# Three two-bank PSUM slots, token sums per batch, a gate in steps and expert pages begun ahead of w2: one change to a linear-attention and expert-routing kernel

## The chip, the cores and the metric

The kernel runs on one core of a Trainium2 chip. Times are microseconds (us) on the device. A kernel is timed several times and the median counts; each timed kernel runs on the same chip as the kernel before, in turns. Each set of runs fell on one of several chips, and the kernel before needs 514 to 516 us on some of them and 519 to 520 us on others.

Engine names as in the profile: PE is TensorE's matmul stream and PEld its weight loads, DVE is VectorE, ACT is ScalarE, POOL is GpSimd, SP is SyncE. A name with a q behind it (SPq, ACTq) is that engine's queue when it issues a transfer. L156 is line 156 of the kernel that is shown. The clock (PEclk) is the granted share of TensorE's full clock.

## The reference, cut to what matters

Attention with random features comes first (batch 8, 8 heads, 576 tokens, head dimension 64, 128 features). Its output, 4608 tokens of 512, goes through a gate that picks one of 8 experts for each token, where a token may have to stay with the expert of the token before it. Then come that expert's two layers.

```python
def phi(x):                                   # x: q or k, scaled
    h = x @ omega.T - sum(x * x) / 2
    return exp(h - max(h)) / sqrt(m)          # the maximum is over the 128 features of one token and head
kv  = einsum('bhsm,bhsd->bhmd', phi(k), v)    # sums over the 576 tokens of a batch
z   = sum(phi(k), axis=2)
out = einsum('bhsm,bhmd->bhsd', phi(q), kv) / (einsum('bhsm,bhm->bhs', phi(q), z) + 1e-6)
# gate: e = argmax(x @ w_gate), or the expert of the token before, by a local gate
h = maximum(x @ w1[e], 0);  y = p[e] * (h @ w2[e])
```

Two things in it shape the kernel. No Q work of a batch can start before all its tokens are in `kv`. And no token can be routed before the gate has seen the tokens ahead of it, so the tokens are routed in two epochs of four batches each and laid out in pages of 128 tokens of one expert.

## The kernel before

K work goes by pairs of batches, nine units a pair: one for the 64-token remainders of both batches, then four of 128 tokens for each batch. The nine Q units of a pair are woven between the K units of the next pair. The weights w1 and w2 arrive in 64 pieces of 512 KB, each loaded to a staging buffer and cast to bf16 by ACT, POOL or DVE. These are the parts that the change touches (cuts marked `...`):

```python
wst  = pool("wst", 3)                              # staging buffers of the weight pieces
ps_t = pool("ps_t", 2, space=PSUM)                 # transposes: one bank each
ps_p = pool("ps_p", 2, space=PSUM)                 # projections: two banks each
ps_k = pool("ps_k", 2, space=PSUM)                 # token sums, later y: one bank each

def k_tile(kb_r, v_view):                          # one K unit
    tp = ps_t.tile(...)  ; 4 transposes            # PE
    kt = copy(tp)                                  # DVE
    pj = ps_p.tile(...)  ; 4 matmuls               # PE
    mx = reduce_max(pj)                            # DVE  (kmx)
    kp = exp(pj)                                   # ACT
    va = v * exp(-mx)                              # POOL
    return kp, va

def main(bb, r):                                   # unit r of batch bb of the pair
    ...
    kp, va = k_tile(...)
    q_tile(...)                                    # 4 transposes of q, copy by ACT
    kv_acc(kst8["kv"], kp, va, 0, 128, False, r == 3)   # 8 matmuls into two sum banks held over the batch
    if r == 3:
        kv_done(P, bb)                             # copy of the sums, 4 transposes, 8 gate matmuls, 3 small copies

for P in range(1, NP):
    for i in range(9):
        ku[i](); qu[i](); load_w(1, "AP")          # K unit, Q unit of the pair before, one piece of w1
    if P == 2: gates[0] = gate(0)                  # routing of the first epoch, in one block
    if P == 3: scatter(*gates[0])                  # 18 indirect writes of the page list, on POOL
...
for i in range(9): qu[i](); load_w(2, "PA")        # last Q units, w2
load_w(32, "PVA")
gates[1] = gate(1)
for ep in range(2):
    ...                                            # list read, 18 pages: gather (POOL), transpose by DMA (SP),
    for i in range(18): page(...)                  # layer 1, relu (ACT), 8 transposes, layer 2, write-back (POOL)
rest(0)                                            # overflow pages, behind a register and a branch
```

The softmax here doesn't subtract the row's maximum and nothing guards it: scores larger than these inputs give would overflow.

## Time and profile before

| | kernel before |
|---|---|
| median, all its runs beside the changed kernel | 514.38 us (4 runs, 513.25 to 515.57) |
| span of the profiled run | 511.2 us |
| busy: PE, DVE, ACT, POOL | 62%, 41%, 34%, 43% |
| mean granted clock | 0.731 |
| first maximum reduction (kmx) starts | 13.3 us |
| the K units of pairs 1, 2, 3 start (first kmx of each) | 55.1, 112.2, 183.3 us |
| last kmx starts | 237.6 us |
| cast of w2: first starts, last ends | 242.8, 302.6 us |
| last of the 36 regular pages is scaled (y) | 482.3 us |

The kmx records make good marks: there is just one for each of the 36 K units, on one engine, in order. I use them, the first and last w2 cast and the last y to cut every run into the same seven stretches. No engine is anywhere near 100% of the span. The averages hide that the stretches have different limits, so the stretches are what has to be read; the prediction shows them for this kernel.

### The profile page before, as it was taken

Reading aid. Unit: us, or ns where it says so; the run is one execution under the profiler, and the core shown is the slowest. Engines: PE = TensorE matmul, PEld = TensorE weight load, DVE = VectorE, ACT = ScalarE, POOL = GpSimd, SP = SyncE. Lnnn points to the kernel's source line nnn. Section 1 sums busy time; section 2 is a strip of 40 time slices with the busy share of each in tenths; the row PEclk is TensorE's granted clock in tenths of the full one; section 3 lists DMA queues with packets and bytes.
Section 4 is the critical chain, followed back from the end, with each engine's and each line's share of the span. In section 5 each row is a group of like instructions: output and inputs, shape, how many; then the busy total and the mean of one; then the engine's idle time right before and its main releaser. Section 6 shows DMA issues by size and latency. Waiting matters only on the chain.

```text
span 511.2 us, 7103 instructions
## 1 busy us (share of the span) xinstructions
PE 317.5 (62%) x2305; PEld 180.6 (35%) x2305; DVE 209.1 (41%) x504; ACT 172.2 (34%) x267; POOL 221.8 (43%) x222
## 2 busy tenths in 40 slices
PE   1455666657573463385532205759999999999633
PEld 0344434335352342163222202324444444444211
DVE  6334454544557653474447410122333233333202
ACT  1256274646453054345562111012222222222100
POOL 3464343345435048822322137753454545453321
PEclk9999565656575565556555556679999999999958
DMA  9949648967796930240798851143444444443110
GB/s 210 330 165 290 248 160 308 240 229 248 257 268 248 324 127 22 103 146 21 248 318 296 289 162 37 42 115 105 124 127 132 120 127 106 133 121 86 74 37 34
DMA packets 82486, 86.62 MB, mean 169 GB/s; under 512 B 39520, under 2 KB 64608, under 8 KB 82448
## 3 DMA queue, kind: packets, MB, share of 16 engines
q1 hardware_dynamic: 72048, 66.91, 43.4%
q0 software_dynamic: 6112, 14.40, 8.8%
q10 hardware_dynamic: 4288, 4.82, 2.8%
q8 instruction: 22, 0.36, 0.3%
q14 instruction: 16, 0.13, 0.1%
HBM read 67.21 MB, written 14.77 MB: 160 GB/s over the span
## 4 chain that ended last, share of the span: by engine, by line
PE 26%; DMA 10%; issue 9%; POOL 6%; ACT 5%; DVE 2%; POOLq 0%; SPq 0%; ACTq 0%; DVEq 0%
PE kv L626 13%; DMA wstage<-in_moe_w_dram 8%; PE pj L615 7%; PE tp L621 3%; ACT h L618 3%; POOL page_list L535 2%; POOL w_all L121 2%; POOL xg L606 1%; DMA lia<-page_list 1%; PE pj L154 1%; DVE kmx L157 1%; ACT kp L159 1%; ACT qp L265 1%; DMA page_list<-meta,posi 0%; PE kv L175 0%
## 5 line engine op out<-in xcount | busy, mean ns | idle before, releaser
L615 PE MATMUL pj<-w_all,xt 128*128 x304 | 80.3, 401 | 42.9 <-DMA xt<-xg 42.9
L618 ACT ACTIVATE h<-pj 128x1024 bf16<-128x1024 f32 x38 | 38.9, 1024 | 159.2 <-PE pj L615 159.2
L626 PE MATMUL kv<-w_all,ht 128*128 x304 | 75.0, 391 | 5.2 <-DVE ht L623 5.2
L164 POOL TENSOR_TENSOR va<-stage,ek 128x512 bf16<-128x512 f32 x32 | 33.5, 1048 | 80.4 <-ACT ek L162 34.6
L606 POOL DMA_INDIRECT xg<-x_tok,ix x36 | 37.5, 1042 | 51.2 <-DMA xt<-xg 47.6
L121 POOL CAST w_all<-wstage 128x1024 bf16<-128x1024 f32 x30 | 31.3, 1046 | 57.2 <-DMA wstage<-in_moe_w_dram 56.3
L615 PEld LDWEIGHTS <-xt 128*128 128x128 bf16 x304 | 29.6, 102 | 73.6 <-DMA xt<-xg 41.8
L157 DVE TENSOR_REDUCE kmx<-pj 128x8 f32<-128x1024 f32 x36 | 43.9, 1222 | 25.7 <-PE pj L154 24.9
L175 PE MATMUL kv<-va,kp 128*128 128x65 bf16 (+1 forms) x320 | 22.8, 230 | 42.4 <-POOL va L164 41.6
L159 ACT ACTIVATE kp<-pj 128x1024 bf16<-128x1024 f32 x36 | 36.8, 1023 | 36.0 <-DVE kmx L157 35.9
L623 DVE COPY ht<-tp 128x1024 bf16<-128x1024 bf16 x38 | 26.1, 687 | 53.4 <-PE tp L621 53.2
L626 PEld LDWEIGHTS <-ht 128*128 128x128 bf16 x304 | 29.9, 99 | 49.3 <-DVE ht L623 18.7
L535 POOL DMA_INDIRECT page_list<-meta,posi x36 | 35.8, 995 | 24.3 <-DVE meta L523 14.3
L154 PE MATMUL pj<-om_bd,kt 128*128 128x256 bf16 x144 | 35.5, 395 | 14.1 <-ACT kp L159 9.5
L117 ACT CAST w_all<-wstage 128x1024 bf16<-128x1024 f32 x30 | 31.4, 1046 | 34.7 <-DMA wstage<-in_moe_w_dram 31.2
L265 ACT ACTIVATE qp<-pj 128x1024 bf16<-128x1024 f32 x32 | 32.5, 1023 | 20.8 <-PE pj L261 20.8
L175 PEld LDWEIGHTS <-kp 128*128 128x128 bf16 (+1 forms) x320 | 19.6, 120 | 49.3 <-issue 39.1
L629 DVE TENSOR_SCALAR y<-kv,lia 128x512 f32<-128x512 f32 x18 | 13.5, 751 | 48.5 <-PE kv L626 48.5
L245 DVE RECIPROCAL rd<-pj 128x8 f32<-128x8 f32 x36 | 7.3, 203 | 62.1 <-PE pj L275 54.7
L275 PE MATMUL pj<-kvb,qp 128*128 128x74 bf16 x256 | 22.6, 246 | 15.2 <-ACT qp L265 9.6
L629 DVE TENSOR_SCALAR y<-kv,lib 128x512 f32<-128x512 f32 x18 | 13.5, 751 | 37.1 <-PE kv L626 37.1
L171 ACT COPY qt<-tp 128x512 bf16<-128x512 bf16 x32 | 18.6, 589 | 26.7 <-PE tp L170 26.6
(181 smaller groups left out, 463.2 us busy)
## 6 DMA issues: line engine op xcount, KB each, us to landing
wstage<-in_moe_w_dram SPq DMA_DIRECT2D x64, 512.0 KB, 4.7
stage<-in_k_dram SPq DMA_DIRECT2D x8, 1024.0 KB, 7.3
stage<-in_q_dram SPq DMA_DIRECT2D x8, 1024.0 KB, 8.8
stage<-in_v_dram SPq DMA_DIRECT2D x8, 1024.0 KB, 11.1
x_tok<-xr ACTq DMA_DIRECT2D x16, 256.0 KB, 4.4
str_k<-in_k_dram SPq DMA_DIRECT2D x8, 128.0 KB, 4.0
str_q<-in_q_dram SPq DMA_DIRECT2D x8, 128.0 KB, 4.2
str_v<-in_v_dram SPq DMA_DIRECT2D x8, 128.0 KB, 4.4
```

Of the source, the lines that this page charges most:

```text
L121: nc.gpsimd.tensor_copy(dst, st)
L154: nc.tensor.matmul(pj[:, 2 * hp:2 * hp + 2, :].rearrange("p a d -> p (a d)"), lhsT=kt[:, hp], rhs=om_bd, start=True, stop=True)
L157: nc.vector.tensor_reduce(mx, pj, axis=AX, op=Alu.max)
L159: nc.scalar.activation(kp, pj, Act.Exp, scale=scale)
L164: nc.gpsimd.tensor_tensor(va[:, :, 0:Dh], v_view, ek.to_broadcast([128, 8, Dh]), op=Alu.mult)
L175: nc.tensor.matmul(kv[h // 4][:, (h % 4) * 65:(h % 4) * 65 + 65], lhsT=kp[lo:lo + n, h, :], rhs=va[lo:lo + n, h, :], start=first and h % 4 ...
L265: nc.scalar.activation(qp, pj, Act.Exp, scale=scale)
L535: s_ = nc.gpsimd.indirect_dma_start(out=plist, out_offset=bass.IndirectOffsetOnAxis(ap=posi[:, t:t + 1], axis=0), in_=meta[:, t, :], in_of ...
L606: nc.gpsimd.indirect_dma_start(out=xg, out_offset=None, in_=src, in_offset=bass.IndirectOffsetOnAxis(ap=ix[:, i:i + 1], axis=0), bounds_ch ...
L615: nc.tensor.matmul(h_ps[:, c, :], lhsT=xt[:, dc, :], rhs=w1_all[:, ds(ev + (dc * F + c * 512), 512)], start=(dc == 0), stop=(dc == DC - 1))
L618: nc.scalar.activation(h, h_ps.rearrange("p a (f c) -> p (a f) c", c=128), Act.Relu)
L626: nc.tensor.matmul(y_ps, lhsT=ht[:, f], rhs=w2_all[:, ds(ev + f * D, D)], start=(f == 0), stop=(f == FC - 1))
```

## The change

Its intent: a third slot for projections, so that PE waits less for evacuations; token sums made in one go after a batch, so that PE doesn't stand at a sum after every unit; the gate's chain of small steps hidden among K and Q units; the scatters hidden under the w2 load; and the first expert layer of some pages, which needs only w1, ahead of the rest of w2. The core of the diff (the gate's other `yield`s, renamed helpers and moved lines are cut):

```diff
-    wst = pool("wst", 3)
-    ps_t = pool("ps_t", 2, space=bass.MemoryType.PSUM)
-    ps_p = pool("ps_p", 2, space=bass.MemoryType.PSUM)
-    ps_k = pool("ps_k", 2, space=bass.MemoryType.PSUM)
+    wst = pool("wst", 2)
+    ps_t = pool("ps_t", 1, space=bass.MemoryType.PSUM)
+    ps_p = pool("ps_p", 3, space=bass.MemoryType.PSUM)
+    ps_k = pool("ps_k", 1, space=bass.MemoryType.PSUM)
...
-    def kv_acc(kv, kp, va, lo, n, first, last):
-        for h in range(H): ...
+    def kv_half(tiles, g):
+        kv = ps_k.tile([128, 4, Dh + 1], F32, name="kv")
+        for i, (kp, va, lo, n) in enumerate(tiles):
+            for h in range(4):
+                nc.tensor.matmul(kv[:, h, :], lhsT=kp[lo:lo + n, 4 * g + h, :], rhs=va[lo:lo + n, 4 * g + h, :], ...)
+        return kv
...
             for g in range(2):
-                nc.scalar.copy(kvb[:, 4 * g:4 * g + 4, 0:65], kv[g][:, 0:260]...)
+                nc.scalar.copy(kvb[:, 4 * g:4 * g + 4, 0:Dh + 1], kv_half(tiles, g))
...
-        return [rem] + [main(bb, r) for bb in range(2) for r in range(4)]
+        return [main(0, r) for r in range(4)] + [rem] + [main(1, r) for r in range(4)]
...
-    load_pair_rem(0)
     load_main(0)
...
+        if P == 3:
+            ga = gate(0)                       # now a generator
...
-            load_w(1, WENG)
+            load_w(1 if P < 3 else 2, "P")
+            if P == 3:
+                next(ga, None)
+                next(ga, None)
...
         qu[i]()
-        load_w(2, "PA")
-    load_w(32, "PVA")
+        load_w(4, "PAV")
+        scatter(0, 2 * i)
+        scatter(0, 2 * i + 1)
...
+    for i in range(NEP):
+        queue.append((lia, i) + hidden(fetch(i, [ixa_], [x_tok[0]]), eia, i))   # first layer
+        for _ in range(3):
+            next(gb_, None)                    # gate(1)
+        out_one(WH - i // 4)                   # second layer, WH = 7 pages behind at most
+        if i >= 5:
+            for t in range(2 * (i - 5), min(2 * (i - 5) + 2, 18)):
+                scatter(1, t)
```

The second layer's y moves from the sum banks to a projection slot. `kp` and `va` get six buffers, since all units of a batch are now kept until its sums.

## The prediction

> **What bounds the kernel now.** I read the page's slices first, then a table of busy time by stage, then the chain of waits, then the waits of TensorE (PE). The slices show three regimes.
>
> ```profile
> PE   1455666657573463385532205759999999999633
> PEclk9999565656575565556555556679999999999958
> DMA  9949648967796930240798851143444444443110
> ```
>
> One digit is 12.8 us. In the first 24 PE is half busy at half clock and no engine is full; from about slice 26 PE is 90% busy or more at full clock: those are the expert pages, which are PE-bound. I cut the run at the marks that instructions give: phase 0 (K only) to 56, pairs 1 and 2 of K with Q to 107 and 160, the routing gate alone to 181, pair 3 to 243, the Q tail to 268, the rest of the w2 load to 302, a slow start of the pages to 340, full pages to 482, overflow pages.
>
> ```profile
> core 0: us, PE busy (x) PEld busy (x) DVE busy (x) ACT busy (x) POOL busy (x), PEclk, DMA share, GB/s
> 13.00:56.00 43.00, 23.72 (x218) 17.15 (x217) 17.21 (x25) 19.41 (x43) 19.70 (x17) 0.92 0.90 276
> 56.00:107.00 51.00, 31.40 (x304) 21.25 (x303) 25.51 (x56) 28.43 (x51) 22.25 (x20) 0.57 0.75 237
> 107.00:160.00 53.00, 33.90 (x336) 22.62 (x334) 27.68 (x62) 29.13 (x53) 22.82 (x21) 0.60 0.80 255
> 160.00:181.00 21.00, 8.29 (x58) 7.09 (x56) 16.03 (x60) 1.92 (x4) 5.42 (x4) 0.50 0.68 231
> 181.00:243.00 62.00, 33.66 (x322) 21.97 (x319) 30.68 (x71) 30.15 (x54) 34.23 (x33) 0.56 0.25 86
> 243.00:268.00 25.00, 11.25 (x126) 6.26 (x124) 11.84 (x37) 14.41 (x16) 7.12 (x7) 0.50 0.86 286
> 268.00:302.00 34.00, 6.11 (x32) 5.45 (x32) 17.05 (x73) 7.98 (x9) 6.71 (x7) 0.50 0.84 278
> 302.00:340.00 38.00, 18.13 (x74) 7.78 (x75) 5.22 (x11) 4.10 (x4) 27.83 (x28) 0.68 0.25 59
> 340.00:482.00 142.00, 139.08 (x791) 65.47 (x790) 46.10 (x66) 32.78 (x32) 63.73 (x62) 0.98 0.41 114
> ```
>
> Three stretches do little for their length. 160 to 181: the gate, DVE 16 of 21 us, nothing beside it. 243 to 302: 32 pieces of w2, DMA 85% busy, PE waiting for the data. 302 to 340: GpSimd (POOL) 28 of 38 us busy with list scatters and gathers while pages drip in. Pair 3 took 62 us against 51 and 53, with POOL up by 12 us: the 18 scatters of the first epoch. The chain agrees for w2 and after; it could be followed back only to 205.5 us.
>
> ```profile
> 268.47 5.96 DMA wstage<-in_moe_w_dram
> 274.48 1.05 POOL w_all L121
> ...
> 297.08 4.62 DMA lia<-page_list
> ```
>
> Each w2 piece is a transfer of 4 to 6 us and then a cast, and the first page waits for a list read issued behind all of them. PE's waits name what the change goes for:
>
> ```profile
> PE pj L615 <- DMA xt<-xg: 42.9, 4, 23.7
> PE kv L175 <- POOL va L164: 41.6, 24, 6.0
> ```
>
> The first is the page start. In the second an in-order PE sits at a token-sum matmul until POOL has scaled v; 18.9 of the 41.6 us fall in pair 3, behind the scatters, 12.4 in phase 0, only 5.9 and 4.4 in pairs 1 and 2.
>
> **What the Trainium skill says.** "Perfetto Trace Analysis", Optimization Strategy, advises interleaving regimes that have different limits; gate, scatter, w2 load and first layer are such regimes, and the table shows them one after another. The same section says that a repeating bubble can mean that PSUM has no room for the next tile. "TensorE: Matmul & The Clock Gate", Part 1, says that the clock is half or full and that idle windows bring it down; the trace agrees (0.50 to 0.60 in K/Q, 0.98 in the pages). "PSUM — Partial Sum Buffer", PSUM bank collisions, says that two engines may not be in one bank at once; so a one-bank slot makes its writer and reader take turns. After the change all eight banks are 1 transpose + 3x2 projection + 1 sum bank. "DMA: Bandwidth & Descriptors", Anatomy of one DMA, fits (for GpSimd-issued transfers) 2.0 us + bytes/436 GB/s: 3.2 us for 512 KB. These are issued by SyncE, yet the shortest w2 landing here is 3.4 us; the median with three in flight is 4.7.
>
> **The change part by part.**
>
> *Gate and scatters moved.* The gate's 21 us leave the path and its DVE work goes between units of pair 3. DVE was 31 of 62 us there, so it has room, but the in-order engines meet chains of PE and DVE: I charge 8 us. The scatters (1.0 us plus 0.3 of issue, 18 of them, 23 us) go to the Q tail, where POOL is 7 of 25 busy beside w2. Pair 3 then resembles pair 2.
>
> *Three slots, sums late.* A K unit holds a slot for 1.0 (matmuls) + 1.2 (max) + 1.0 (exp), a Q projection 0.6 + 1.0, a numerator 0.7 + 1.1: 6.6 us per unit pair, 3.3 on two slots, 2.2 on three. Measured are 51/9 = 5.7 and 53/9 = 5.9, so slots are not the only limit; ordering is. PE is idle 20 of 51 us. Waits for a slot and for va in pair 2 add up to about 12 us of PE; if half goes, pairs 1 and 2 take 45 and 46. DMA bounds it from below: 0.75x51 = 38 and 0.80x53 = 42 us. Phase 0 has DMA at 0.90, so little more than 2 us is to be had there, though 12.4 us of va waits vanish. Against it: one transpose bank, shared by K and Q transposes and their two copies (0.6+0.4+0.6+0.6 = 2.2 us of each unit, under 5), and one sum bank, where two rounds of 20 matmuls with a 0.4 us copy take turns. All w1 casts go to POOL: 32x1.04 = 33 us instead of half; its load per pair becomes some 28 of 46 us, no bound. Sum for the end of K: 54 + 45 + 46 + (46+8) = 199 us, against 243.
>
> *w2 with two staging buffers.* Now 59 us for 32 pieces, 1.8 each: three in flight. With two, one piece takes 3.4 to 3.9 landing + 1.0 cast (0.7 on DVE, a third of them) + 0.1 or 0.2, about 4.9, halved 2.45: 78 us. This part costs 19 us. w2 complete at 199+78 = 277, against 302.
>
> *First layer ahead.* A page costs 4.2 us of PE (two periods of the chain are 8.4), of which the first layer and its transposes are 8x0.215+0.62 = 2.35. The loop lets eight first layers run before the first output. Even at half clock they need under 40 us of PE, and the Q tail should end 25 to 35 us after K, so most fit into the w2 window. Left then: 38x4.2 - 8x2.35 = 141 us. The second epoch's scatters now go two per page: 2.6+1.3+1.3 = 5.3 us of POOL against 4.2 for about six pages; with restarts I charge 7. Last page 277+141+7 = 425.
>
> *End.* Overflow pages still wait for a register and a branch: 511-482 = 29 us, unchanged: span 454. The timed run is 2.5 us above the span here (513.7 against 511.2; the profiled execution itself was timed at 513.4): about 456.
>
> **The rivals.**
> 1. The list read and the page transposes stay behind all w2 transfers in SyncE's queue, so nothing runs ahead. For: that is how the before trace reads, list read at 297 after the last w2 issue at 296. Against: the queue isn't in source order everywhere: a stage load went out at 50.1, ahead of w1 pieces written before it that went at 70.4. This adds 19 us and a start of 4.6+0.9+2.9+2.7 = 11: 486.
> 2. The single transpose and sum banks become what the missing slot was, and K/Q keeps 52 us per pair: +6+6+6, 474. For: PE already waits for transpose evacuation at times. Against: those waits are 1 or 2 us per pair.
> 3. DMA takes over in K/Q, with w1 staging halved and blocking POOL before the casts of k and q: 2 to 4 us a pair, 465.
> 4. w2 casts sit behind scatters and Q work on in-order engines and a piece takes 3 us: 96 us instead of 78, 474.
> 5. Better: with fewer gaps PE stays warm, pairs come to their DMA floor (38 to 42) and w2 takes 2.2 a piece: 12+8 us less, 436.
>
> **Range and chances.** The gate, the scatters and the page start are idle stretches worth some 60 us together, and the code takes all three apart; the staging buffer gives 19 back. Any one rival leaves the change faster; rivals 1, 2 and 4 together come to about 520. I choose 456, range 434 to 484: faster by over 2% 0.94, within 0.04, slower 0.02.
>
> **What would show it.** K's last max reduction near 195 rather than 238; no stretch with DVE alone; no wait of PE for va of over 10 us in total; w2 pieces 2.4 us apart; first-layer matmuls before the last w2 cast, about eight pages; page period 4.2 as before; the end still 29 us. Wrong it would be if the pairs still take 52 us, if the first page matmul follows the last w2 cast, or if w2 pieces are over 3 us apart.

## The result, and the profile after

The changed kernel takes 496.0 us (median of 4 runs, 495.54 to 496.88), the kernel before 514.38 us beside it. The ratio is 0.9644, with a 95% interval of 0.9616 to 0.9673. A ratio here is the mean time of one kernel's runs over that of the other's of the same rounds, so it isn't quite the ratio of the two medians. The change is faster by over 2%, which was given a chance of 0.94. It is 40 us slower than the 456 predicted, and outside the range of 434 to 484.

The slices of the profile's page for the changed kernel (span 494.1 us, one digit is 12.35 us), to be set against the first lines shown in the prediction:

```profile
PE   0356576657656465833723970059999999999543
PEclk9999997565556576575555796559999999999858
DMA  9977488587965899320677965563454544453210
```

The three regimes are still there. The full pages begin at slice 28, as before, which is 333 us now and was 345. The gate's slices (13 and 14) have PE at 6 and 4, where they had 3 and 4. Under the w2 load there is now PE work (9 and 7 in slices 23 and 24), and then a hole (0 and 0).

The table of busy time by stage, of the changed kernel: the two pairs 65 to 118 and 118 to 175, the rest of the K units, the stretch without one, and the w2 load behind the Q tail:

```profile
core 0: us, PE busy (x) PEld busy (x) DVE busy (x) ACT busy (x) POOL busy (x), PEclk, DMA share, GB/s
65.00:118.00 53.00, 33.36 (x332) 23.27 (x331) 27.32 (x60) 25.55 (x49) 25.69 (x23) 0.68 0.74 228
118.00:175.00 57.00, 35.80 (x351) 25.51 (x349) 35.38 (x90) 25.91 (x50) 28.89 (x26) 0.56 0.82 251
175.00:222.00 47.00, 27.62 (x276) 20.63 (x275) 30.54 (x90) 22.24 (x42) 24.86 (x24) 0.68 0.58 177
222.00:236.00 14.00, 5.41 (x74) 4.04 (x72) 2.55 (x5) 5.14 (x8) 11.08 (x12) 0.50 0.06 11
...
254.00:334.00 80.00, 33.76 (x162) 17.61 (x163) 27.08 (x87) 16.17 (x17) 39.82 (x39) 0.63 0.68 196
```

Pair 1 takes 53 us, where it took 57 before, with 33 us of PE work. Nothing is full in it. From 222 to 236 POOL is busy for 11 of 14 us and DMA stands still. The w2 stretch has DMA at 0.68, where the kernel before had 0.85.

The same seven stretches, predicted and measured, tell where the 40 us are:

| stretch | before | predicted | changed kernel |
|---|---|---|---|
| start to first kmx of pair 1 | 55.1 | 54 | 65.3 |
| pair 1 | 57.1 | 45 | 53.4 |
| pair 2 (before: with the gate) | 71.1 | 46 | 56.7 |
| pair 3 to the first w2 cast (predicted: with the gate's 8) | 59.5 | 54 | 60.9 |
| w2 load, first cast to end of last | 59.8 | 78 | 97.7 |
| then to the last y of 36 | 179.7 | 148 | 130.7 |
| end | 28.9 | 29 | 29.4 |
| sum | 511.2 | 454 | 494.1 |

The K phase ends 37 us later than predicted, the w2 load takes 20 us more, and the pages give 17 back. (The predicted column ends K at 199, the measured one at the first w2 cast, 236.3; the last kmx itself is at 222.5.) The columns don't start from quite the same marks: the prediction cut pair 1 at 107 us, inside the gap between its last kmx (102.2) and the first of pair 2 (112.2), and so read 51 us where these marks give 57.1. Set against what each stretch took before, the forecast up to the first w2 cast was -2, -6, -28 and -8 us, and +10, -4, -14 and +1 were measured.

**Where the pairs lose time.** PE's waits over the whole run of the changed kernel, the two largest:

```profile
PE kv L180 <- POOL va L166: 41.3, 20, 7.5
PE pj L648 <- POOL w_all L122: 25.4, 1, 25.4
```

The wait for `va` was 41.6 us before the change and is 41.3 after. In this profile making the sums late has not removed it; it has gathered it from 24 places into 20: 5.7 us up to the first kmx of pair 1 (12.4 before), 8.5 in pair 1 (5.9), 9.4 in pair 2 (4.4) and 17.7 in the rest of K (18.9). The amount isn't steady: a second profile of the changed kernel (g2 below) has 32.3 us. The second line is the hole in front of the pages: one wait of 25.4 us, at the first second-layer matmul, for a w2 cast on POOL.

What the third slot does can be read in pair 1. PE's waits for a projection slot add up to 10.7 us before (55.1 to 112.2 us) and to 2.1 after (65.3 to 118.7). But the wait for `va` has grown. Before, in that stretch:

```profile
PE kv L175 <- POOL va L164: 5.9, 5, 1.8
```

And after:

```profile
PE kv L180 <- POOL va L166: 8.5, 7, 2.1
```

The wait of the projections for `kt` has grown too, from 0.5 to 3.6 us.

The kmx starts show the pattern. Within a batch a unit comes every 4.2 us in pair 1 (5.3 before). But twice a pair, where the sums of a batch are made, there is a gap: 82.8 to 94.7 and 106.7 to 118.7 us, 12 us each. The kernel before had 10 us there (77.8 to 88.0 and 102.2 to 112.2). This is one of these gaps, from the timeline of the changed kernel (start, duration, engine, line, operation, output and inputs, and in brackets the idle time before it and what ended it):

```profile
85.77 1.04 POOL L166 TENSOR_TENSOR va<-str_v,ek 128x512 bf16<-128x512 f32 x1 [3.43 <-ACT ek L164]
...
86.86 0.37 PE L180 MATMUL kv<-va,kp 64*128 64x65 bf16 x4 [1.70 <-POOL va L166]
...
87.27 0.38 ACT L220 CAST kvb<-kv 128x260 bf16<-128x260 f32 x1 [0.57 <-PE kv L180]
...
88.58 1.89 POOL L207 CAST qb<-stage 128x2048 bf16<-128x2048 f32 x1
...
89.11 0.38 ACT L220 CAST kvb<-kv 128x260 bf16<-128x260 f32 x1 [1.46 <-PE kv L180]
89.53 1.10 DVE L224 COPY kvc<-kvb 128x512 bf16<-128x512 bf16 x1 [0.50 <-ACT kvb L220]
...
90.68 0.61 PE L226 MATMUL tp<-ident_bf,kvc 128*128 128x128 bf16 x4 [1.61 <-DVE kvc L224]
...
91.81 0.38 PE L232 MATMUL tp<-wgbd,kvt 128*128 128x18 bf16 x8 [0.52 <-DVE kvt L228]
...
92.52 0.58 PE L151 MATMUL tp<-ident_bf,kb 128*128 128x128 bf16 x4 [0.33 <-DVE kvb L235]
```

This is one serial chain: v scaled, first half of the sums, its copy out of the one sum bank, second half, its copy, a copy for the transposes, the transposes in the one transpose bank, their copy, the gate matmuls in the same bank, their copy, and only then, at 92.52, the next K unit's transposes, which need that bank too (their releaser is the last copy, kvb). The chain itself isn't new: in e4 below, with two transpose and two sum banks, the same steps fill the gap at this place, 11.1 us long. On the way DVE's `kvc` copy takes 1.10 us, against 0.29 for the fastest of its kind in this kernel. It ends 0.16 us after POOL's cast of `qb`, which ran from 88.58 to 90.47. The Trainium skill ("SBUF — State Buffer", Who interferes with whom) says that VectorE and GpSimd share a pair of ports, and that an operation of the one that needs the pair waits for the whole operation of the other. The trace agrees: eight of these copies have a median of 0.90 us here and 0.29 before.

**The start.** The first kmx comes at 20.4 us instead of 13.3. DVE waits 6.3 us, until 9.84, for the gate's weights, two small loads that land 5.7 and 7.9 us after issue (3.3 and 3.9 before). Dropping the remainder loads from the front has put 3 MB of stage loads in the first 4 us. Then DVE meets POOL's first big casts. From the timeline of the changed kernel:

```profile
13.81 1.89 POOL L205 CAST kb<-stage 128x2048 bf16<-128x2048 f32 x1
...
13.94 1.80 DVE L478 TENSOR_SCALAR pm<-gi 128x50 f32<-128x50 f32 x1
...
15.64 1.89 POOL L207 CAST qb<-stage 128x2048 bf16<-128x2048 f32 x1
15.66 1.91 DVE L541 TENSOR_SCALAR meta<-ids 128x18 int32<-128x18 int32 x1
```

Each of two tiny DVE operations lasts as long as the cast beside it; before, they took 0.52 and 0.63 us.

**The end of K.** From the timeline of the changed kernel, around the first w2 cast:

```profile
231.47 0.97 POOL L552 DMA_INDIRECT page_list<-meta,posi  x1 [0.30 <-issue]
232.44 1.08 POOL L166 TENSOR_TENSOR va<-stage,ek 128x512 bf16<-128x512 f32 x1
233.58 0.71 PE L180 MATMUL kv<-va,kp 128*128 128x65 bf16 x8 [7.47 <-POOL va L166]
...
236.31 0.70 DVE L120 CAST w_all<-wstage 128x1024 bf16<-128x1024 f32 x1 [9.74 <-PE kv L180]
```

The last `va` stands behind a row of first-epoch scatters in POOL's queue, PE waits 7.5 us for it, and the first cast of w2 waits 9.7 us, since w2 takes the memory of the K buffers.

**The w2 load.** The first twelve casts come 2.5 us apart, as predicted (236.3 to 264). The other twenty come 3.4 us apart. The two largest waits of SP's queue between 264 and 334 us in the changed kernel:

```profile
SPq L625 <- DMA xg<-x_tok,ix: 17.3, 8, 4.5
SPq L112 <- POOL w_all L122: 14.3, 4, 5.2
```

SP issues both the w2 transfers (L112) and the page transposes (L625), in order. For 17.3 us it stands at a transpose whose gather hasn't landed, and for 14.3 us at a staging buffer whose cast sits in POOL's queue among scatters and gathers.

### The profile page after: what moved, and what is told of

It is laid out like the page before. It is cut to its first block, busy times and chain, and to the rows that moved or that the text cites. A ratio compares the mean times of both kernels' runs of the same rounds, so it can differ in the third digit from the quotient of the medians.

```text
span 494.1 us, 7017 instructions
## 1 busy us (share of the span) xinstructions
PE 311.5 (63%) x2305; PEld 180.8 (37%) x2305; DVE 212.7 (43%) x511; ACT 155.1 (31%) x247; POOL 233.5 (47%) x235
## 4 chain that ended last, share of the span: by engine, by line
PE 20%; issue 11%; DMA 8%; ACT 5%; POOL 5%; DVE 2%; POOLq 0%; SPq 0%; ACTq 0%; DVEq 0%
PE pj L634 10%; ACT h L637 5%; PE pj L648 5%; DMA wstage<-in_moe_w_dram 4%; PE tp L640 3%; POOL page_list L552 2%; DMA xt<-xg 2%; DMA xg<-x_tok,ix 2%; POOL out_dram L652 1%; POOL w_all L122 1%; POOL xg L621 1%; DVE sel L440 1%; DMA out_dram<-y,lib 1%; ACT w_all L118 0%; PE kv L180 0%
## 5 line engine op out<-in xcount | busy, mean ns | idle before, releaser
L648 PE MATMUL pj<-w_all,ht 128*128 x304 | 77.1, 384 | 25.4 <-POOL w_all L122 25.4
L122 POOL CAST w_all<-wstage 128x1024 bf16<-128x1024 f32 x43 | 44.7, 1046 | 39.3 <-DMA wstage<-in_moe_w_dram 39.3
L180 PE MATMUL kv<-va,kp 128*128 128x65 bf16 (+1 forms) x320 | 25.5, 237 | 44.2 <-POOL va L166 41.3
L634 PEld LDWEIGHTS <-xt 128*128 128x128 bf16 x304 | 31.4, 104 | 53.7 <-DMA xt<-xg 12.6
L648 PEld LDWEIGHTS <-ht 128*128 128x128 bf16 x304 | 28.7, 99 | 55.2 <-issue 27.4
L180 PEld LDWEIGHTS <-kp 128*128 128x128 bf16 (+1 forms) x320 | 22.0, 124 | 49.9 <-issue 31.2
L640 PE MATMUL tp<-ident_bf,h 128*128 128x128 bf16 x304 | 24.5, 225 | 10.1 <-DVE ht L642 5.6
L640 PEld LDWEIGHTS <-h 128*128 128x128 bf16 x304 | 18.3, 100 | 27.2 <-ACT h L637 21.8
L652 POOL DMA_INDIRECT out_dram<-y,lib x18 | 17.8, 991 | 19.5 <-DVE y L651 16.2
L156 PEld LDWEIGHTS <-kt 128*128 128x128 bf16 x144 | 16.2, 130 | 27.5 <-DVE kt L153 22.7
L120 DVE CAST w_all<-wstage 128x1024 bf16<-128x1024 f32 x11 | 8.0, 730 | 41.8 <-DMA wstage<-in_moe_w_dram 32.1
```

Source lines behind the costliest of these rows:

```text
L122: nc.gpsimd.tensor_copy(dst, st)
L156: nc.tensor.matmul(pj[:, 2 * hp:2 * hp + 2, :].rearrange("p a d -> p (a d)"), lhsT=kt[:, hp], rhs=om_bd, start=True, stop=True)
L180: nc.tensor.matmul(kv[:, h, :], lhsT=kp[lo:lo + n, 4 * g + h, :], rhs=va[lo:lo + n, 4 * g + h, :], start=(i == 0 and h == 0), stop=(i == l ...
L634: nc.tensor.matmul(h_ps[:, c, :], lhsT=xt[:, dc, :], rhs=w1_all[:, ds(ev + (dc * F + c * 512), 512)], start=(dc == 0), stop=(dc == DC - 1))
L640: nc.tensor.transpose(tp[:, f], h[:, f], ident_bf)
L648: nc.tensor.matmul(y_ps[:, 0, :], lhsT=ht[:, f], rhs=w2_all[:, ds(ev + f * D, D)], start=(f == 0), stop=(f == FC - 1))
```

## The experiments

All of them ran correct. They start from the changed kernel unless said otherwise. Marks are read from one profile of each run. How far they can be trusted shows in g2, the changed kernel profiled once more on another chip: the first kmx of pairs 1 and 2 came within 1.3 us of the first profile's, but the first w2 cast 5.5 us and the end of the load 7.5 us later. Differences of that size, late in the run, prove nothing. One run of the kernel before, of 951.51 us, was an outlier.

### Batch ends and PSUM banks

**e1_sums_late**: the sums of a batch one unit later.

```diff
-            kv_done(0)
+            kst8["due"] = lambda: kv_done(0)      # called in the next unit, after its tiles
```

> Edit: the token sums of a batch (and what hangs on them: copies, transposes, gate weights) are emitted one K unit later, after the next unit's transposes and projection; the rest of the change stays. Theory A (the end of a batch is a serial chain through the one sum bank and the one transpose bank, and the next unit's transposes stand behind it): the gap between the max reductions at a batch end falls from about 12 us to 5 to 7, six or seven times, so K ends 30 to 40 us earlier and the kernel takes 456 to 470 us. Rival B (K/Q is paced by its transfers and by GpSimd's casts of k and q for the next batch, whatever the order of the sums): the gap stays at 10 us or more and the time within 5 us of 496.

Measured: 492.61 us, before 519.19, ratio 0.9506 (0.9478 to 0.9533). The last kmx is at 214.6, 8 us earlier. The gaps have moved by one unit (54.8 to 65.0, 76.3 to 85.5) and are 9 to 10 us instead of 12. So the place of the sums is worth something, but moving them doesn't close the gaps. That the chain keeps the one transpose bank and the one sum bank wherever it stands is argued here, not shown.

**e5_late_kvps**: e1, with the chain's transposes and gate matmuls in a projection slot.

```diff
-            kvt_ps = ps_t.tile([128, 4, 128], BF, name="tp")
+            kvt_ps = ps_p.tile([128, 4, 128], BF, name="pj")
-            g_ps = ps_t.tile([128, 8, E + 1], F32, name="tp")
+            g_ps = ps_p.tile([128, 8, E + 1], F32, name="pj")
```

> Edit: as the run with late sums, and the two PSUM tiles of the chain after the sums (transposed sums, gate weights) come from the three projection slots, not from the single transpose bank. Theory A (what stops K at a batch end is the next unit's transposes standing behind the chain in the single transpose bank): the gap at batch ends falls from 8 to 10 us to under 7, K's last max reduction comes at 205 us or earlier (214.6 in the run with late sums), ratio to the kernel before 0.92 to 0.94. Rival A2 (the chain's own work on in-order engines stops K, whichever bank it uses): gaps stay at 8 to 10 us, ratio 0.945 to 0.955.

Measured: 487.39 us, before 514.49, ratio 0.9469 (0.9417 to 0.9522); last kmx 214.2, gaps still 10 us (55.2 to 65.4, 77.5 to 87.2). Taking the chain out of the transpose bank alone doesn't close them.

**e4_banks222**: two transpose banks, two projection slots, two sum banks, as before the change; all else as changed.

```diff
-    ps_t = pool("ps_t", 1, ...)   ps_p = pool("ps_p", 3, ...)   ps_k = pool("ps_k", 1, ...)
+    ps_t = pool("ps_t", 2, ...)   ps_p = pool("ps_p", 2, ...)   ps_k = pool("ps_k", 2, ...)
-        y_ps = ps_p.tile([128, 2, 512], F32, name="pj")
+        y_ps = ps_k.tile([128, D], F32, name="kv")
```

> Edit: PSUM as before the change (two transpose banks, two projection slots, two sum banks, page outputs in a sum bank), all else of the change kept. Theory A's third slot is worth what the K units gained (4.2 us instead of 5.7 between two reductions inside a batch, some 20 units: 25 to 30 us), and two transpose and sum banks give back some of the batch ends (2 to 4 us each, 8 times): net 0 to 15 us slower, 496 to 511. Rival (the single banks cost more than the third slot gives): faster than 490.

Measured: 485.16 us, before 519.19, ratio 0.9345 (0.9318 to 0.9372), faster than the changed kernel. Phase 0 goes at 39.0 us from first kmx to that of pair 1, not 44.9; the pairs take 53.1 and 50.6 us, not 53.4 and 56.7; the last kmx is at 207.4 instead of 222.5. In phase 0 of the changed kernel the units inside a batch come 3.24 to 3.31 us apart, 2.8 on average in e4: the turn of the one transpose bank from K to Q and back. The K transposes of a unit wait until ACT has copied the Q transposes of the unit before out of that bank:

```profile
24.72 0.59 PE L151 MATMUL tp<-ident_bf,kb 128*128 128x128 bf16 x4 [0.37 <-ACT qt L173]
```

After it, in the K units of pair 1, third slot and single banks nearly cancel: within a batch, three slots and single banks take 29.5 us for the two batches, pairs of banks 32.6; at the two batch ends they take 24.0 and 20.5. In pair 2 the units inside the batches take 29.6 us either way, and the two ends 27.1 and 21.0, the second of them with the gate's first steps, which use the sum bank too. So pairs of banks shorten the batch ends, but to 9.4 to 11.1 us, not away. The wait for `va` falls to 27.8 us. e4 also moves y to a sum bank, and eleven first layers get as far as their relu before its w2 load ends (eight in the changed kernel, the eighth in the load's last us); this part of the edit isn't separated.

**e9_banks_acc**: e4 with the sums made unit by unit as before the change, the gate's small tiles in the transpose banks.

```diff
+                else:
+                    acc_tile(0, kst8[0][-1], r == 0, False)    # 8 matmuls after each unit, two banks held
```

> Edit: PSUM as before (the fourth run) and the token sums accumulated unit by unit as before, instead of in two halves at the end of a batch; the gate's small tiles in the transpose banks as before; order of units, gate steps, run-ahead and casts as in the change. If the late sums are what keeps the batch ends at 9 to 11 us, they fall by 2 us each and K ends 10 to 16 us earlier than in the fourth run: ratio 0.905 to 0.92. If late sums took waits for v off TensorE inside the batch as the change means, undoing them makes the units slower: ratio 0.94 to 0.955.

Measured: 494.49 us, before 515.54, ratio 0.961 (0.9541 to 0.9679); last kmx 212.9. It is 9 us slower than e4, or 2 to 3% by the ratios. But pairs 1 and 2 take 52.6 and 51.0 us, as in e4 (53.1 and 50.6): there late sums gain nothing. The loss arises in pair 3, between its first and last kmx (49.3 us, 45.2 in e4), where the gate's steps run, whose tiles this edit moves as well. So the 2 to 3% can't be put down to the sums alone. And the pairs are shorter here than in the changed kernel (53.4 and 56.7), with neither its slots nor its late sums.

**f4_banks_late**: e4 and e1 together.

```diff
+    ps_t, ps_p, ps_k = 2, 2, 2 buffers; y in ps_k                  # as in e4
+            kst8["due"] = lambda: kv_done(0)                        # as in e1
```

> Pairs of banks (as in e4) and the sums of a batch one unit later (as in e1). If the single banks and the place of the sums are two separate causes, the gaps at the batch's ends shrink under the 9 to 10 us that each alone left, the last maximum reduction falls below 205 and the ratio to 0.92 to 0.93. If the batch's end is one chain of dependent steps that the next unit of the same batch has to wait for wherever it stands, the ratio stays at 0.93 to 0.94.

Measured: 478.1 us, before 519.0, ratio 0.9207 (0.917 to 0.9244). The ratio is where two separate causes were expected to put it, and the gaps after the sums are 7.6 to 9.1 us in pairs 1 and 2. Pairs 1 and 2 start at 54.1 and 102.7 (58.6 and 111.6 in e4), and pair 3 at 150.4, 12 us earlier than in e4. But the last kmx, at 208.0, isn't below 205: with K that far ahead, the scatters fall among the last units (POOL is busy 40 of the 58 us from 150 to 208). 12 us of lead become 3 at the first w2 cast (219.3 against 222.4), and 8 again at its end.

### The parts that were expected to pay

**e6_gate_block**: the first epoch's gate in one block before pair 3.

```diff
-            ga = gate(0)
+            for _ in gate(0):
+                pass
```

> Edit: the first epoch's gate in one block at the head of pair 3, as before the change; all else of the change kept. If stepping the gate is what took its 15 to 18 us off the path, the max reductions of pair 3 shift by 12 to 18 us and the ratio goes from 0.964 to 0.985 to 1.0. Rival (the gate's work costs the same spread out, since its engines are in order): ratio within 0.006 of 0.964.

Measured: 505.65 us, before 514.49, ratio 0.9814 (0.976 to 0.9868); the last kmx at 235.4, 13 us later. Against 496.0 on a chip of like speed (514.38 for the kernel before), the steps are worth 9.7 us, give or take some 3 by the intervals.

**e7_no_ahead**: second layers at most two pages behind the first.

```diff
-        out_one(WH - i // 4)
+        out_one(2)
```

> Edit: outputs follow two pages behind the first layers from the start, so three first layers run before the wait for w2 instead of seven. If running ahead is worth its PE time, four first layers of 2.35 us warm are lost, 9 to 10 us: ratio 0.98 to 0.985. Rival (running ahead costs the w2 load what it gains, through page transposes in the same queue): ratio within 0.006 of 0.964 and a w2 load shorter than 98 us by 8 us or more.

Measured: 505.44 us, before 514.49, ratio 0.9845 (0.9765 to 0.9925). Three first layers run under the w2 load instead of seven, and PE's wait for w2 is 44.5 us instead of 25.4. Running ahead is worth 9.4 us, give or take some 4. The w2 load itself is the same (235.4 to 333.0), so the number of pages ahead isn't what stretches it.

### The w2 load

**e2_wst3**: three staging buffers (and one `xr` buffer less, for room).

```diff
-    wst = pool("wst", 2)
+    wst = pool("wst", 3)
```

> Edit: three staging buffers for the weights, as before the change (the x output tile has two buffers instead of three to make room). Theory C (w2 is slowed by the third staging buffer that was taken away): the w2 load falls from 98 us to 70 to 78, the time to 472 to 480. Rival D (w2 pieces stand behind list scatters, gathers and page transposes in the in-order queues, and a third buffer doesn't help): the load stays above 90 us, the time within 5 us of 496.

Measured: 512.68 us, before 519.19, ratio 0.9887 (0.9863 to 0.9912). The w2 load takes 58.4 us (236.6 to 295.0), as before the change. But SP's queue now has 29 w2 pieces in a row until 290, the list read at 290.3 and the first transposes from 298.7: nothing runs ahead, the first layer comes at 306. This is the prediction's first rival, brought about by the third buffer.

**e3_scat1_late**: the second epoch's scatters from page 9 on, not 5.

```diff
-        if i >= 5:
-            for t in range(2 * (i - 5), min(2 * (i - 5) + 2, 18)):
+        if i >= 9:
+            for t in range(2 * (i - 9), min(2 * (i - 9) + 2, 18)):
```

> Edit: the list scatters of the second epoch start after page 9 of the first layer instead of page 5, so that none falls between the w2 casts. Rival D: the w2 load falls by 15 to 20 us (18 scatters of 1.3 us, on the engine that casts a third of the pieces), time 476 to 484. Theory C (staging buffers alone): w2 load within 5 us of 98, time within 6 us of 496.

Measured: 498.08 us, before 519.19, ratio 0.9621 (0.9576 to 0.9667). SP's wait for POOL's casts after 264 us falls from 14.3 to 3.7 us, and the load still ends at 335.8. The scatters alone aren't the cause.

**e8_wst3_act**: three staging buffers, list reads and page transposes issued by ACT.

```diff
-        nc.sync.dma_start_transpose(out=xt, in_=xg)
+        nc.scalar.dma_start_transpose(out=xt, in_=xg)
```

> Edit: three staging buffers as in the second run, and the list reads and page transposes are issued from ScalarE's queue instead of SyncE's. Theory C2 (two buffers slow w2 to 98 us, and with three the first layers fell behind because their transposes and the list read were put behind all w2 issues on SyncE): the w2 load takes 58 to 66 us and at least four first layers start before the last w2 cast; ratio 0.89 to 0.93. Rival (on ScalarE they fall behind the casts as they did on SyncE, or the pages are slowed): no first layer before the last cast, ratio 0.97 to 1.0.

Measured: 492.13 us, before 514.49, ratio 0.9503 (0.9436 to 0.957), of two runs (487.5 and 489.45 us) and two over 1.5% slower, among which the profiled one. In that profile the load takes 91 us (238.0 to 328.6); its largest SP wait after 264 us is 18.6 us for ACT's casts, which now sit behind the transposes.

**e10_w2_split**: e8, with all w2 casts on DVE.

```diff
-        load_w(4, "PAV")
+        load_w(4, "V")
```

> Edit: three staging buffers, all w2 casts on VectorE, list reads and page transposes issued from ScalarE: SyncE then carries only w2 issues, GpSimd only gathers and scatters, and no queue carries both the load and the pages. Theory C3 (the w2 load is long because loads, casts and pages share in-order queues): the load takes 58 to 68 us and seven first layers still run before its end; w2 complete at 300 instead of 334, last page 25 to 33 us earlier: ratio 0.90 to 0.92. Rival (transfers bound it): over 80 us, ratio 0.94 to 0.97.

Measured: 492.88 us, before 515.54, ratio 0.9507 (0.9449 to 0.9565). The load takes 81 us (234.9 to 316.0), and the last y is still at 464: between 317 and 350 the pages starve, as it looks behind the second epoch's scatters, which fill POOL there.

**e11_banks_scat0**: e4, with the first epoch's scatters held until the last `va`.

```diff
+        with tc.issue_after(kst8["va"].ins):
             scatter(0, 2 * i)
```

> Edit: PSUM as before (the fourth run), and the scatters of the first epoch are held behind the last multiplication of v on GpSimd. If K's end waits for v behind scatters (15 us from the last max reduction to the first w2 cast), that stretch falls to 6 to 8 us: ratio 0.915 to 0.925. Rival (the scatters then delay the w2 casts and the list read by as much): 0.930 to 0.940.

Measured: 487.78 us, before 515.54, ratio 0.9472 (0.943 to 0.9514). The stretch from the last kmx to the first w2 cast shrinks from 15 to 6 us (210.8 to 216.8), but the load ends at 332.6, where e4's ended at 331.5, and the whole is no faster (by the ratio it is 1.3% slower than e4). What is won before the load is lost in it.

**e12_banks_w2_split**: e4 and e10 together.

```diff
+    ps_t, ps_p, ps_k = 2, 2, 2 buffers; y in ps_k                  # as in e4
+    wst = pool("wst", 3); load_w(4, "V"); nc.scalar.dma_start_transpose(...)   # as in e10
```

> Edit: PSUM as before, and the tenth run's three edits together. If the K part (15 us) and the w2 part (25 to 33 us) add up: ratio 0.875 to 0.895. If they share the same slack: 0.90 to 0.92.

Measured: 494.78 us, before 515.54, ratio 0.958 (0.9525 to 0.9636). The load ends at 303.2, 28 us earlier than e4's, and the last y comes at 463.7, 9 us later. A piece of the timeline of this run:

```profile
313.60 0.97 POOL L552 DMA_INDIRECT page_list<-meta,posi  x1 [0.30 <-issue]
314.88 0.97 POOL L552 DMA_INDIRECT page_list<-meta,posi  x1 [0.30 <-issue]
316.16 0.97 POOL L552 DMA_INDIRECT page_list<-meta,posi  x1 [0.30 <-issue]
```

One scatter every 1.28 us, nine in a row here, and 18 of them from 308 to 338 us, with only a gather now and then: this looks like what took the load's place.

**f1_banks_w2_pin**: e12, with the scatters two per page, each pair after a page's gather.

```diff
-        if i >= 5:
-            for t in range(2 * (i - 5), ...): scatter(1, t)
+        if i >= 8:
+            with tc.issue_after(kst8["xg"].ins):
+                for t in range(2 * (i - 8), ...): scatter(1, t)
```

> Pairs of banks everywhere (as in e4) with the w2 split of e12 (three staging buffers, casts on VectorE, list reads and page transposes on ScalarE), and the second epoch's scatters spread two per page after the page's gathers from page 8 on, so that they can no longer clump on GpSimd between 308 and 337 us. Theory A (in e12 the clump of scatters on GpSimd took the place of the shortened w2 load): first layers and pages run on through 305 to 340, the last y falls to 445 to 452, about 475 us, ratio 0.915 to 0.93. Rival B (something else, such as gate(1) on VectorE or the landing of the gathers, holds the pages at 335 anyway): last y stays at 455 to 465, ratio 0.94 to 0.96.

Measured: 494.58 us, before 519.0, ratio 0.9543 (0.95 to 0.9586); last y at 461.9. The clump is gone and the time has not moved, so the clump alone was not the cause. PE's one large wait between 304 and 355 us in this run:

```profile
PE tp L640 <- ACT h L637: 15.7, 6, 4.3
```

ACT computes `h` in 1.02 us, but in this version it also issues the page transposes, in order, and each of these waits for a gather. The pages come 7 to 9 us apart from 317 to 340. As I read it, moving the transposes to ACT freed the w2 load and put the same waits on the path of the pages; no run separates this from the scatters, which still fill much of POOL's time here.

**f2_all**: f1, the first epoch's scatters held as in e11, and the gate weights loaded first as in f3.

```diff
+        with tc.issue_after(kst8["va"].ins): scatter(0, ...)        # as in e11
+    nc.sync.dma_start(out=wgf[:, :, 0:E], ...)                      # as in f3
```

> f1 plus the first epoch's scatters held behind the last v multiply (as in e11) plus the gate weights loaded ahead of the token stages on SyncE. Theory A: another 5 us at the start and up to 8 us between the last maximum reduction and the first w2 cast, about 465 us, ratio 0.895 to 0.915. Rival B: as in e11, what is won before the w2 load is lost in it, ratio 0.93 to 0.95.

Measured: 484.84 us, before 519.0, ratio 0.9359 (0.9314 to 0.9404). The first kmx is at 12.0 instead of 21.5, the last at 201.0 instead of 212.1, the load ends at 290.9 instead of 303.0, and the last y is at 451.6 instead of 461.9. The start's gain carries through to the end; that of the held scatters doesn't.

### The start, a control, and the fastest version

**f3_gate_weights_first**: the gate weights' loads issued by SP, ahead of its stage loads.

```diff
-    nc.scalar.dma_start(out=wgf[:, :, 0:E], ...)
+    nc.sync.dma_start(out=wgf[:, :, 0:E], ...)
```

> The changed kernel with only the gate weights' loads issued ahead of the token stages on SyncE. If the 7.1 us by which its first maximum reduction comes later than before (20.4 against 13.3) is the gate weights waiting behind 3 MB of stage loads, the first maximum reduction falls to 14 to 17 us, and the whole by some 4 to 6: about 491 us, ratio 0.952 to 0.958. Rival: the stage loads themselves come later by as much, the first maximum reduction stays at 19 to 21 and the ratio at 0.962 to 0.967.

Measured: 494.67 us, before 519.0, ratio 0.9542 (0.9501 to 0.9584). The first kmx falls to 12.2 us: the start was indeed the gate weights behind the stage loads. Against the first profile of the changed kernel the lead of 8.2 us is 4.3 at the last kmx (218.2), 0.3 at the first w2 cast (236.0) and 1.2 at the last; against its second (g2) it is 5.8, 5.8 and 8.7. So whether the start's gain is lost later isn't settled by these marks.

**g2_changed_again**: the changed kernel once more, unedited.

> The changed kernel itself, unedited, beside g1 on one chip, as a control: kernel before was 514 us on two chips and 519 on two others, so ratios of different calls may differ by a per cent. If the changed kernel moves with the chip as before does, its ratio is 0.962 to 0.967 here too; if only before is slower on some chips, the ratio is 0.954 to 0.958 on a chip where before takes 519.

Measured: 498.95 us, before 519.75, ratio 0.9593 (0.9537 to 0.9649), between the two expectations. So ratios of different chips can be compared to about half a per cent, no closer, and f3's gain over the changed kernel is unclear.

**g1_best**: f4 with f3's edit.

```diff
+    ps_t, ps_p, ps_k = 2, 2, 2 buffers; y in ps_k                  # as in e4
+            kst8["due"] = lambda: kv_done(0)                        # as in e1
+    nc.sync.dma_start(out=wgf[:, :, 0:E], ...)                      # as in f3
```

> Pairs of banks, sums one unit later (as in f4) and the gate weights loaded ahead of the token stages (as in f3). f3's trace ended only 1.6 us earlier than the changed kernel's, although its first maximum reduction came 8 us earlier. If what is won at the start is lost again wherever the transfers set the pace, g1 is 1 to 3 us below f4's 478; if it was lost at f3's single banks, g1 is 5 to 8 us below, about 471.

Measured: 469.62 us, before 519.75, ratio 0.9029 (0.8967 to 0.9091). It is 29 us faster than the changed kernel on the same chip (498.95), and 50 us faster than the kernel before. Against f4's marks, the first kmx is 7.7 us earlier, pair 3 7.4, the last kmx 7.3, the end of the w2 load 7.3 and the span 7.7. With the banks in pairs the start's gain is kept. Whether the single banks lost it isn't shown: f3 is 4.3 us faster than g2 (494.67 and 498.95, the kernel before 519.0 and 519.75), of 8 gained at the start. Its stretches: 46.8 to the first kmx of pair 1, pairs of 48.5 and 47.7, then 68.9, 104.1 for w2, 122.4 and 30.3. The load of w2 is 6 us longer than in the changed kernel, and the whole is the fastest. In g1, as in e4 and f4, eleven first layers get as far as their relu before the load ends.

## Why the prediction was right or wrong, point by point

**"Three slots, sums late": this step failed, and it is the main one.** It took 6 and 7 us off pairs 1 and 2 (51 to 45, 53 to 46) and put the end of K at 199 us, on the ground that half of some 12 us of waits for a slot and for `va` would go (in pair 2 the trace has 14). The slot waits did go, from 10.7 to 2.1 us in pair 1. But the waits for `va` and `kt` grew by 2.6 and 3.1 us there, pair 1 fell by 4 us only, and pair 2 takes 57 us, more than the 53 that the prediction had read. Not even the 4 us can be credited to this step: e9, with slots, banks and sums as before and the rest of the change, has pairs of 52.6 and 51.0 us. So third slot, single banks and late sums together gained nothing in pair 1 and lost some us in pair 2, where 6 and 7 had been forecast. One profile could mislead here, but the runs agree: with the change's banks and order (the changed kernel, e2, e3, e6, e7, e8, e10, f3, g2) pair 1 takes 50.3 to 56.4 us and pair 2 53.5 to 57.2; with pairs of banks (e4, e11, e12, f1, f2) they take 52.6 to 54.2 and 50.6 to 52.4. What makes e9's pair 1 shorter than the 57.1 before (the order of the units, w1 casts on POOL alone, more `kp` and `va` buffers) isn't separated.

The price of the change, single transpose and sum banks, was rated at nothing because the sum of the copies (2.2 us of a unit) is under 5 us. That sum was right, and the wrong thing to look at. A single bank makes its users take turns along a chain of dependent steps: a turn of the transpose bank takes 3.24 us, and the gaps at the batch ends of pairs 1 and 2 are 11.9 to 15.1 us. Most of such a gap is the chain itself, which is there with pairs of banks too (9.4 to 11.1 us in e4, 10 before); the single banks add 1 to 4 us to each. e4 shows the balance: giving the third slot back for the second banks makes the kernel faster by 11 to 14 us (485.16 against 496.0 and 498.95). It has the first w2 cast at 222.4 us and g1 at 211.9, so that of the 37 us that K lost against the prediction, e4 takes 14 back and g1 24. The rest isn't assigned. The prediction's second rival ("the single transpose and sum banks become what the missing slot was") is what happened, and its figure of 474 was still too low, because a start, a w2 load and a gate that had been rated too favourably stood under it.

**The wait for `va` was to fall under 10 us in all.** It didn't: 41.6 us before, 41.3 and 32.3 in two profiles after. With the sums one unit later still, or with the banks in pairs, it is 22.4 to 27.8 us (e1, e4, f4, g1), and in these runs K is shorter. Late sums alone moved the wait to the batch ends and left the part behind the scatters in pair 3 (18.9 and 17.7 us); e11, which is e4 with the scatters held back, has 18.7 us in all where e4 has 27.8.

**Phase 0, "little more than 2 us is to be had".** It became 10 us longer. 7 us are the start, where the gate weights queue behind 3 MB: f3 shows this cause. The rest goes with the single banks (e4: 39.0 instead of 44.9 us from first kmx to pair 1), inside the batches with the turn of the transpose bank. The prediction hadn't looked at what moving the first remainder loads would do.

**"Gate and scatters moved".** The gate in steps is worth 9.7 us (e6), where the prediction had 21 − 8 = 13. The scatters were supposed to go to the Q tail "beside w2"; some stand in front of the last `va` instead, and 14 us pass between the last kmx and the first w2 cast. e11 removed that delay and won nothing, since the load then took longer.

**"w2 with two staging buffers": 2.45 us a piece.** 2.5 were measured for the first twelve pieces, and 3.4 for the other twenty: 97.7 us instead of 78. The prediction's fourth rival had the size (96 us) by another cause, casts behind scatters. What the runs show is that transfers, transposes, casts, gathers and scatters share the in-order queues of SP, POOL and ACT. Later scatters (e3) and fewer pages ahead (e7) don't shorten the load alone. A third buffer with the transposes elsewhere does (91, 81 and 77 us in e8, e10, e12), and then the pages wait for what was moved. How much of the 20 us belongs to each of them is not settled.

**"First layer ahead".** It works, and e7 puts its worth at 9.4 us. Seven ran, not eight: the prediction misread the loop, in which `out_one(WH - i // 4)` lets the queue hold six at page 7. The estimate for the rest, 148 us, was too high by 17. It took 38 pages, although the last two are overflow pages and already in the 29 us of the end. With this and the seven put right: 36 × 4.17 − 7 × 2.35 = 134. And the 7 us for the second epoch's scatters were not paid there, since these ran under the w2 load. The page period of 4.2 us and the end of 29 us were right.

**What the prediction named as signs of being wrong** came true: pairs of over 52 us, and w2 pieces over 3 us apart on average. The chance of 0.94 for faster was right for the reasons given: the gate's stretch and the page start were both taken apart, for 9.7 and 9.4 us. Range and point were wrong because the rivals were weighed one at a time, while two of them came together. Rivals 2 and 4 added to the 456 make 492, near the measured 496; that they come so near is luck, since the start came 11 us later than forecast and the pages gave 17 back.

Smaller readings of the prediction: the full pages begin in slice 28 of its page, not 26. And the 3.2 us for 512 KB that it sets beside the landings is an estimate from the fit in the Trainium skill ("DMA: Bandwidth & Descriptors", Anatomy of one DMA); of the 64 weight pieces before the change the quickest took 3.2 us to land and the median 4.7.

## What to carry to other kernels

Before banks are moved from one role to another, the chain of dependent steps that will pass through the role that is left with one bank has to be written down end to end, with what must wait at its far end; adding up busy times of that bank doesn't show it. When two streams of work are laid side by side, count how many in-order queues they share, and be ready to find that freeing one of them hands the wait to the next, as it looks in e11, e12 and f1. And try the parts of a large change one at a time: here the gate in steps and the run-ahead were each a gain of about 2%, the new bank split a loss of about 3%, the late sums no gain in the pairs for which they were made, and the version with pairs of banks, sums one unit later and the gate's weights loaded first is 6% faster than the change as made.

## What the Trainium skill lacked or had wrong

- "SBUF — State Buffer", Who interferes with whom: right, and of more weight here than I had thought. It speaks of operations measured slower, but doesn't say how this looks in a profile, namely as busy time of the blocked engine: a 128x50 operation of DVE reads 1.80 us beside a POOL cast of 1.89 (0.52 before), and a 128x512 copy has a median of 0.90 us instead of 0.29.
- "PSUM — Partial Sum Buffer" has the bank rules, but I found nothing there on how to divide the eight banks between roles. Here 2/2/2 slots against 1/3/1 of the same eight banks are 11 to 14 us of 496.
- "Perfetto Trace Analysis", Optimization Strategy: a repeating bubble "can mean" too little PSUM. Here one projection slot more, paid for with transpose and sum banks, left the bubble at the batch ends at 12 us (10 before). Its advice to interleave regimes held (9.7 and 9.4 us for two of them), without a word that the regimes' in-order queues are then shared, which goes with the w2 load's 97.7 us instead of 59.8.
- "DMA: Bandwidth & Descriptors" gives the time of one DMA alone and an HBM latency under load, but no figure for a small load beside large ones. Two small loads issued beside 3 MB of others landed after 5.7 and 7.9 us, not 3.3 and 3.9; issuing them first on the other queue brought the first kmx from 20.4 to 12.2 us.
